# Strassen quads for v and z2, attention during the x load, and engine orders fixed at build time by a clock model

## The chip, the cores and the metric

The kernel runs on one core of one Trainium2 chip. The metric is the device time of one execution in microseconds (us). Times are medians of three or more executions. A ratio is the mean time of one kernel's runs over the mean of the other's runs of the same rounds, so it is not quite the ratio of the medians quoted beside it.

The engines are called as the profile calls them: PE is the tensor engine, PEld its weight loads, DVE the vector engine, ACT the scalar engine, SP the engine that issues most DMAs.

## The reference

The output is a gated mix of two branches over the same x (2048 rows, 1024 columns).

```python
# cut: random inputs; A_x (1, 2048, 1024), wqkv (1024, 3072), w_in (1024, 3584),
# w_sp (2048, 2048), w_out (1792, 1024): z1 and z2 have FH = 1792 columns each
g = _sigmoid((x * gate_w).sum(-1, keepdims=True))
a = _A_ref(x, A_wqkv, A_wo)                          # 32 heads of 32, local attention
b = _B_ref(x, B_w_in, B_w_sp, B_b_sp, B_w_out)
return g * a + (1 - g) * b

# _A_ref: q, k, v = x @ wqkv; every position attends to itself and to the 7 positions
# 2, 4, ... 14 before it; softmax of 8 logits; o @ wo
# _B_ref: z = gelu(x @ w_in); z1, z2 = halves of z; z2 = layernorm(z2);
# b = (z1 * (w_sp @ z2 + b_sp)) @ w_out
```

## The kernel before

The work in PE's order is: transposes of the first x tiles and a first quarter of z2 while x is still landing; the gate; for eight groups of four heads q and k, and the band products q·k of a group between them; v; the rest of z2; then z1, the spatial product and the output product. The last three were already done by Strassen's scheme, 7 products for 8; one such set of 7 is called a "quad" below. Attention after the bands is DVE's: it waits for the group's rows of logits, which go from SBUF to a DRAM scratch (`band_d`) and come back in another layout (`att_L`).

```python
# the products that the change replaces (cut: stores, counters)

    def z2_tile(i, c, bank=next_bank):
        N = ZC + 1 if c == 0 else ZC
        ps = bank()
        for kt in range(KT):
            nc.tensor.matmul(ps[:, 0:N], xT[:, kt, i * P:(i + 1) * P], w2[:, kt, w2_off[c]:w2_off[c] + N],
                             start=(kt == 0), stop=(kt == KT - 1))
    # ... cut

    def v_tile(hf, j):
        ps = low_bank()
        for kt in range(KT):
            nc.tensor.matmul(ps[:], _sub_ap(xT_flat, kt * S + j, [[NJ, P]]), wv[:, kt, 512 * hf:512 * hf + 512],
                             start=(kt == 0), stop=(kt == KT - 1))
        st = vst_slots[(j // 4) % 2]
    # ... cut: the v tile is copied by ACT and stored to v_d

# the band products and the copies that free their banks (cut: the loops over blocks and heads)
                    nc.tensor.matmul(banks[4 + h][QB * q:QB * (q + 1), m * KW + skip:(m + 1) * KW], qt[hp, e, at:at + QB],
                                     kt_[hp, e, at - (W - 1) + skip:at + QB], start=True, stop=True,
                                     tile_position=(DH * h, QB * q), skip_group_check=True)
    # ...
        evac = nc.scalar.copy(dst, src)
    # ... then DMAs from SBUF to band_d

# softmax of one group: rows come back, maxima on DVE, exponential on ACT
    def attend1(g):
        L = att_L[g % 2]
        L4 = L[:].rearrange("p (j u h) -> p j u h", j=NJ, u=W)
        bd = band_d[g]
        for e in range(2):
            sync.dma_start(L[:, 256 * e:256 * e + 256].rearrange("p (j x) -> p j x", j=8),
                           bass.AP(tensor=bd.tensor, offset=bd.offset + 16 * e * BS, ap=[[8 * (BR + HG), P], [BR + HG, 8], [1, W * HG]]))
        tt = nc.vector.tensor_tensor
        tt(att_m[:], L4[:, :, 0:4, :], L4[:, :, 4:8, :], ALU.max)
        tt(att_m[:, :, 0:2, :], att_m[:, :, 0:2, :], att_m[:, :, 2:4, :], ALU.max)
        tt(att_m[:, :, 0:1, :], att_m[:, :, 0:1, :], att_m[:, :, 1:2, :], ALU.max)
        last_sub[0] = tt(L4, L4, att_m[:, :, 0:1, :].to_broadcast([P, NJ, W, HG]), ALU.subtract)
        exps[g] = nc.scalar.activation(L[:], L[:], ACT.Exp, scale=float(SCALE))
        if EXP_AFTER[g] < len(evacs):
            tc.add_manual_dep(exps[g].ins, evacs[EXP_AFTER[g]].ins.name, NOSYNC, reason="by then its logits are there")
```

`EXP_AFTER` is a hand-written list: the exponential of group g stands in ACT's order at the 20th, 27th, 51st ... copy that ACT makes. Everything else in the engine orders before z1 is left to the scheduler.

## Time and profile before

| | before |
|---|---|
| median of 3 runs | 683.04 us (682.75 to 685.5) |
| profiled span | 680.2 us |
| PE busy | 665.4 us, 98% |
| first z1 product | 289.1 us |
| all that PE waited for anything | about 9 us, 5.8 of it for the first x rows |

From the page of the kernel before: busy times, PE's busy tenths in 40 equal slices of the span, the clock granted to PE in tenths, and the chain of waits.

```profile
span 680.2 us, 10313 instructions
...
PE 665.4 (98%) x4075; PEld 323.0 (47%) x4135; DVE 407.4 (60%) x551; ACT 289.5 (43%) x547; POOL 6.1 (1%) x15
...
PE   6999999999999999999999999999999999999997
...
PEclk9999999999999999999999999999999999999999
...
## 4 chain that ended last, share of the span: by engine, by line
PE 95%; DMA 2%; issue 1%; DVE 1%; SPq 1%; ACT 0%; ACTq 0%; DVEq 0%
```

From PE's waits, kernel before (what was waited for: us in total, times, longest).

```profile
engine line waited for: us in total, times, longest us
PE psum_all L202 <- DMA arena<-in_A_x_dram: 5.8, 2, 3.5
```

PE is the limit everywhere: it is busy in every slice, its clock is full, and it is 95% of the chain. Beyond the 9 us of waits, nothing but less PE work can shorten this kernel. From PE's timeline, kernel before, round the start of z1 (start us, us, operation, count):

```profile
start us, us, engine line op out<-in xcount [idle before <-releaser]
267.78 20.40 PE L232 MATMUL psum_all<-arena 128*128 128x448 bf16 x107
...
289.10 3.18 PE L474 MATMUL psum_all<-arena 128*128 128x512 bf16 x14
```

A run of 107 products of 448 columns takes 20.40 us, 0.191 each; PE goes from z2 into z1 without a gap. (Some matmul records are missing from the trace, so counts there can be short by a few per cent.)

### The profile page before, as it was taken

How to read it: one execution, taken by the hardware profiler on the slowest of the kernel's cores; microseconds unless marked ns; L12 is line 12 of the kernel's file. 1: busy time of each engine (PE TensorE's matmuls, PEld its weight loads, DVE VectorE, ACT ScalarE, POOL GpSimd, SP SyncE). 2: the span in 40 equal slices, each digit the busy share in tenths (PEclk: the TensorE clock that was granted, in tenths of full speed). 3: DMA queues.
4: the chain of work that ended last, by engine and by line, in shares of the span. 5: the costliest groups of instructions: out<-in, count | busy, mean ns of one | idle time of the engine just before them, and what ended most of it. 6: DMA issues, size and time to landing. Idle time of an engine off the chain costs nothing.

```text
span 680.2 us, 10313 instructions
## 1 busy us (share of the span) xinstructions
PE 665.4 (98%) x4075; PEld 323.0 (47%) x4135; DVE 407.4 (60%) x551; ACT 289.5 (43%) x547; POOL 6.1 (1%) x15
## 2 busy tenths in 40 slices
PE   6999999999999999999999999999999999999997
PEld 3544654466444555544444444444444444444443
DVE  1000119899199989866769766888676695333301
ACT  4435634624566889677866311212112122222221
POOL 1000000000000000000100000000000000000000
PEclk9999999999999999999999999999999999999999
DMA  9995654764666470138894587648356299944100
GB/s 232 225 277 116 139 137 116 167 172 94 155 177 154 126 163 1 52 104 191 210 187 155 140 195 153 151 129 255 95 149 167 67 208 187 212 106 98 46 32 31
DMA packets 241743, 98.12 MB, mean 144 GB/s; under 512 B 189712, under 2 KB 235168, under 8 KB 241696
## 3 DMA queue, kind: packets, MB, share of 16 engines
q1 hardware_dynamic: 241008, 96.94, 58.2%
q8 instruction: 32, 0.52, 0.3%
q10 hardware_dynamic: 688, 0.53, 0.2%
q14 instruction: 15, 0.12, 0.1%
HBM read 45.10 MB, written 36.61 MB: 120 GB/s over the span
## 4 chain that ended last, share of the span: by engine, by line
PE 95%; DMA 2%; issue 1%; DVE 1%; SPq 1%; ACT 0%; ACTq 0%; DVEq 0%
PE psum_all L474 56%; PE psum_all L272 16%; PE psum_all L232 15%; PE psum_all L280 6%; PE psum_all L312 2%; DMA band_d_71<-arena 1%; DMA arena<-in_A_x_dram 1%; SPq L184 0%; DMA arena<-o_d 0%; DMA v_d<-arena 0%; PE psum_all L202 0%; DVE arena L685 0%; ACT arena L283 0%; DVE arena L680 0%; DVE arena L525 0%
## 5 line engine op out<-in xcount | busy, mean ns | idle before, releaser
L474 PE MATMUL psum_all<-arena 128*128 128x512 f16 (+1 forms) x1758 | 385.6, 379 | 2.0 <-DVE arena L685 0.2
L474 PEld LDWEIGHTS <-arena 128*128 128x128 f16 (+1 forms) x1792 | 175.3, 98 | 212.2 <-issue 1.3
L272 PE MATMUL psum_all<-arena 128*128 128x512 bf16 x493 | 111.0, 379 | 2.3 <-issue 1.9
L232 PE MATMUL psum_all<-arena 128*128 128x448 bf16 (+1 forms) x512 | 99.7, 355 | 0.0
L365 DVE TENSOR_TENSOR arena<-arena,att_A 128x8192 f16<-128x8192 bf16 x16 | 70.7, 4420 | 12.1 <-DMA arena<-v_d 12.0
L272 PEld LDWEIGHTS <-arena 128*128 128x128 bf16 x512 | 48.6, 98 | 56.8 <-issue 0.2
L232 PEld LDWEIGHTS <-arena 128*128 128x128 bf16 x512 | 49.8, 98 | 47.0 <-issue 1.5
L365 DVE TENSOR_TENSOR arena<-arena 128x4096 f16<-128x4096 f16 (+2 forms) x48 | 67.3, 1401 | 1.2
L274 ACT CAST arena<-psum_all 128x512 bf16<-128x512 f32 x64 | 37.4, 586 | 53.3 <-PE psum_all L272 53.3
L280 PE MATMUL psum_all<-arena 128*128 128x512 bf16 x249 | 55.4, 379 | 0.9 <-issue 0.4
L483 ACT COPY psum_all<-psum_all 128x512 f32<-128x512 f32 x36 | 20.5, 570 | 80.7 <-PE psum_all L474 80.7
L523 DVE TENSOR_TENSOR arena<-arena 128x512 f16<-128x512 bf16 (+2 forms) x37 | 20.7, 568 | 42.1 <-PE psum_all L474 30.9
L234 ACT ACTIVATE arena<-psum_all 128x448 bf16<-128x448 f32 x64 | 34.7, 547 | 26.2 <-PE psum_all L232 26.0
L280 PEld LDWEIGHTS <-arena 128*128 128x128 bf16 x256 | 36.7, 144 | 18.5 <-issue 0.5
L497 ACT COPY psum_all<-psum_all 128x512 f32<-128x512 f32 x36 | 20.6, 571 | 48.7 <-PE psum_all L474 48.6
L490 ACT COPY psum_all<-psum_all 128x512 f32<-128x512 f32 x36 | 20.5, 570 | 48.6 <-PE psum_all L474 48.3
L590 ACT ACTIVATE arena<-psum_all 128x512 bf16<-128x512 f32 x56 | 31.6, 599 | 7.2 <-DVE psum_all L593 3.7
L319 ACT CAST arena<-psum_all 128x1988 f16<-128x1988 f32 (+1 forms) x24 | 33.7, 1405 | 1.1 <-PE psum_all L312 0.4
L526 DVE TENSOR_TENSOR arena<-arena 128x512 f16<-128x512 bf16 (+2 forms) x37 | 20.6, 566 | 21.2 <-PE psum_all L474 15.5
L338 DVE TENSOR_TENSOR att_m<-att_L_106 128x256 f16<-128x256 f16 x4 | 1.2, 290 | 50.8 <-DMA att_L_106<-band_d_68 32.8
L283 ACT CAST arena<-psum_all 128x512 bf16<-128x512 f32 x32 | 18.4, 587 | 26.5 <-PE psum_all L280 25.9
L487 ACT COPY arena<-psum_all 128x512 f32<-128x512 f32 x22 | 12.8, 587 | 34.5 <-PE psum_all L474 33.7
(87 smaller groups left out, 361.5 us busy)
## 6 DMA issues: line engine op xcount, KB each, us to landing
arena<-v_d SPq DMA_DIRECT2D x8, 960.0 KB, 6.9
z_d<-arena SPq DMA_DIRECT2D x28, 256.0 KB, 2.6
arena<-z_d SPq DMA_DIRECT2D x28, 256.0 KB, 3.3
zg_d<-arena SPq DMA_DIRECT2D x56, 128.0 KB, 2.2
arena<-zg_d SPq DMA_DIRECT2D x32, 224.0 KB, 3.1
arena<-in_A_wqkv_dram SPq DMA_DIRECT2D x16, 256.0 KB, 5.6
v_d<-arena SPq DMA_DIRECT2D x32, 128.0 KB, 2.4
o_d<-arena SPq DMA_DIRECT2D x4, 1024.0 KB, 5.5
```

The lines of the kernel that those rows point to most:

```text
L232: nc.tensor.matmul(ps[:, 0:N], xT[:, kt, i * P:(i + 1) * P], w2[:, kt, w2_off[c]:w2_off[c] + N], start=(kt == 0), stop=(kt == KT - 1))
L234: inst = nc.scalar.activation(z2[:, i, ZC * c:ZC * (c + 1)], ps[:, 0:ZC], ACT.Gelu_apprx_tanh, accum_out=s1[:, 4 * i + c:4 * i + c + 1])
L272: nc.tensor.matmul(ps[:], w[:, t, kt, :], xT[:, kt, 512 * c:512 * (c + 1)], start=(kt == 0), stop=(kt == KT - 1))
L274: inst = nc.scalar.copy(dst[:, :, 256 * c:256 * (c + 1)], ps[:].rearrange("p (n e) -> p e n", e=2))
L280: nc.tensor.matmul(ps[:], _sub_ap(xT_flat, kt * S + j, [[NJ, P]]), wv[:, kt, 512 * hf:512 * hf + 512], start=(kt == 0), stop=(kt == KT - 1))
L319: evac = nc.scalar.copy(dst, src)
L365: inst = nc.vector.tensor_tensor(*a)
L474: nc.tensor.matmul(bank[:], lhsT, rhs, start=(start and m == 0), stop=(stop and m == n - 1), skip_group_check=True)
L497: seed = nc.scalar.copy(V[:], Y[:])
L523: first = nc.vector.tensor_tensor(s_out[0], a21, a22, ALU.add)
L526: nc.vector.tensor_tensor(s_out[2], a11, a21, ALU.subtract)
L590: last_gelu[0] = nc.scalar.activation(z1s[:, f, a, :], bank[:], ACT.Gelu_apprx_tanh)
```

## The change

The intent is to take PE work away. v of groups 3 to 7 and almost all of z2 are now computed by Strassen quads on differences of x tiles. These differences were needed for z1 anyway and are now made at the start and kept. The v of groups 0 to 2 (with the gate column beside it, 385 columns in all) is computed during the x load, together with group 0's q, k and bands, so that attention starts earlier and DVE finds time for the quads' additions. And from the gate on the program is written in the order of a model of the engines, the "clock": every piece of work advances its engine's clock by a guessed duration, DMAs by a guessed issue, transfer and landing time, and the next thing to be written is whatever the model says is ready first. Each instruction is then tied to the one written before it on its engine, so that the scheduler can't move it ("pinned").

The diff is 1261 lines; this is its core. First, the placement of the exponentials and the old v and z2 go, and the model comes (cut marks are "# ..."):

```diff
# ...
-    EXP_AFTER = (20, 27, 51, 60, 83, 93, 103, 117)
# ...
+    pinned = {}
+    traced = [0]
+    due = []
+
+    def settle():
+        ins = nc.cur_bb.bb.instructions
+        for i in ins[traced[0]:]:
+            if i.engine in pinned:
+                if pinned[i.engine] is not None:
+                    tc.add_manual_dep(i, pinned[i.engine], NOSYNC, reason="as it is written")
+                pinned[i.engine] = i.name
+        traced[0] = len(ins)
+
+    def take(engine, dur, ready=0.0):
+        clock[engine] = max(clock[engine], ready) + dur
+        return clock[engine]
# ...
+    def issue(item):
+        if item in due:
+            due.remove(item)
+            ready, dur, f, landed = item
+            sp = take("SP", 0.55, ready)
+            end = take("DMA", dur, sp + 0.6) + 0.5
+            f()
+            if landed is not None:
+                landed(end)
+
# ...
```

The rows of a group are read back (`load_bands`) when the model says that its band stores have landed and DVE is done with the buffer; their landing time sets `t_bands`, which the maxima on DVE wait for in the model, and the end of the maxima sets the exponential's place in ACT's order:

```diff
# ...
+            L4 = att_L[g % 2][:].rearrange("p (j u h) -> p j u h", j=NJ, u=W)
+            yield lambda g=g: t_bands[g], 0.21, lambda: tt(att_m[:], L4[:, :, 0:4, :], L4[:, :, 4:8, :], ALU.max), False
+            yield now, 0.14, lambda: tt(att_m[:, :, 0:2, :], att_m[:, :, 0:2, :], att_m[:, :, 2:4, :], ALU.max), True
+            yield now, 0.11, lambda: tt(att_m[:, :, 0:1, :], att_m[:, :, 0:1, :], att_m[:, :, 1:2, :], ALU.max), True
+            yield now, 0.34, lambda: tt(L4, L4, att_m[:, :, 0:1, :].to_broadcast([P, NJ, W, HG]), ALU.subtract), True
+            sub_end[g] = clock["DVE"]
# ...
+    def next_bands():
+        g = bands_at[0]
+        if g < bands_have[0] and g - weighed[0] < 2 and not any(i in due for s in stored.values() for i in s):
+            dma(max(band_data[g], clock["DVE"] if g > 1 else 0.0), 0.9, lambda: load_bands(g), lambda t: t_bands.__setitem__(g, t))
+            take("SP", 0.6)
+            bands_at[0] += 1
# ...
+            events = [(max(i[0], clock["SP"]), 0, i) for i in due]
+            events += [(sub_end[g], 1, g) for g in range(NG) if sub_end[g] < FAR]
+            events += [(max(o[0], clock["DVE"]) + FR * o[1], 2 + n, o) for n, o in enumerate(options())]
+            events = [v for v in events if v[0] <= t]
# ...
+            elif kind == 1:
+                exp_end[x] = take("ACT", 0.6 + table("exp"), sub_end[x] + 0.1)
+                sub_end[x] = FAR
+                exponential(x)
# ...
```

The weights of z2 are loaded in 16 small DMAs of 112 KB per half, written as 8 events, spread by `gap` on the model's clock, and DVE's weight sums follow their landing:

```diff
# ...
+    def load_later(p, at, gap):
+        land = [0.0]
+
+        def landed(t):
+            land[0] += 1
+            if land[0] == KT:
+                fill.extend((t, 1.05, f) for f in wz_sums(p))
+        for n, f in enumerate(load_wz(p)):
+            dma(at + gap * n, 0.65, f, landed)
# ...
+            next_v()
+            load_later(0, clock["PE"] + 6.0, 3.0)
# ...
+    load_later(1, clock["PE"], 1.2)
+    mark(banks[4:8], ZC)
+    junk = reg(R_OFF + 12288, FH)
# ...
```

And in the start, the gate column's copy (it frees the PSUM bank of a v tile) goes from ACT to DVE:

```diff
# ...
-            nc.scalar.copy(gl_s[:, i:i + 1], ps[:, ZC:ZC + 1])
# ...
+        nc.vector.tensor_copy(gl_s[:, i:i + 1], ps[:, VP:VP + 1])
# ...
```

## The prediction

> **What bounds it now.** The tensor engine: the page shows PE busy 665.4 of 680.2 us, the chain of waits is 95% PE, and the view of waits gives PE only 9 us of waits, 5.8 of them for the first x rows. In the timeline a 512-column matmul costs 0.215 us start to start (1.727 per eight), a 448-column one 0.190 (62.3 us for 328). [...]
>
> **What changes.**
> - z2: 512 matmuls of 448 columns become 420 (15 quads) + 32: 97.3 -> 85.9 us.
> - v: 256 of 512 columns (55 us) become 128 of 385 (20.9) and 224 of 320 (30.5): 51.4 us.
> - Filler matmuls: 4 -> 16, +0.9 us.
> - q/k (110 us), bands, z1, spatial and output products stay.
>
> PE work before z1 falls by about 14 us, all on the critical path: the floor is 669 us.
>
> DVE gets weight sums (8 us for z2) and the bank additions of the v and z2 quads (12 and 22 us). With the attention (8 groups of 17 us of products and 2.5 of softmax) that is about 198 us, to fit in some 218 between its first softmax and z1. It fits because attention starts earlier (first maximum before: 69.9 us; after: 55 to 62). ACT in z1 loses copies and gains squares: neutral.
>
> **What I think is given back.**
> 1. Start, 5 us (2 to 8). In the built order of DVE the eight x differences stand between the tiny copies of the gate column (psum to gl_s) of x tiles 3 to 6, and a sum that waits for the late v weights stands before tile 7's. [...] The differences wait for x tiles 8-11 and 12-15. Transposed x loads are issued 1.62 us apart and land 3.9 us later; with the 512 KB q/k load put between (2.2 us at 232 GB/s), tile 11 lands near 22.5 us and tile 15 near 29. Tile 3's copy holds the bank that the first band products need at about 20 us; tiles 4-7 hold the four low banks. I expect PE to stall some 4 us at 20-25 us and 2 us at 30-37. Before, PE ran without a gap from 15.65 us.
> 2. z1 to spatial, 2 us: the last normalisation stands behind spatial weight sums (2.29 us each), and the first spatial sums behind it.
> 3. 1 us in the v and z2 quads, where an addition waits behind a 2.2 us attention product.
>
> Sum: 683 - 14 + 5 + 2 + 1 = 677 us.
>
> **What would show it.** 0.136 us per 320-column and 0.190 per 448-column matmul; first z1 product near 280 us (289.1 before); spatial and output stages still 167 and 137 us apart from step 2; PE waiting for DVE before 40 us and at the first spatial quad.
>
> **What would make it wrong.** If x lands sooner, the start costs nothing: 670. If DVE falls behind its fixed order in the z2 quads, or a store fixed behind a late load holds a band buffer, stalls add up to 683 or worse. [...]
>
> 677 us, range 670 to 683.5; chances 0.09 faster, 0.89 within 2%, 0.02 slower.

The 0.136 and 0.163 us of the new widths: scaling the 0.190 us of 448 columns by width, an estimate, gives the same two (0.190 x 320 / 448 and 0.190 x 385 / 448), so v comes to 128 x 0.163 + 224 x 0.136 = 51.4 us, and the 14 us are 11.4 of z2 and 3.6 of v, less 0.9 for the fillers.

## More of the kernel before

The kernel before was timed again beside every experiment, on three chips, and had medians of 682.5 to 684.25 us there; where half a per cent matters, read the ratios.

A band set's product fills four PSUM banks, and ACT has to copy them out before the next set may start. This copy and the exponential of the softmax are both ACT's.

## The result, and the profile after

| | before | after |
|---|---|---|
| median | 683.48 us (682.75 to 685.5, 4 runs) | 701.37 us (699.57 to 704.21, 4 runs) |
| ratio | | 1.0262, 95% interval 1.0232 to 1.0293 |
| profiled span | 680.2 us | 699.1 us |
| PE busy | 665.4 us | 663.4 us |
| DVE busy | 407.4 us | 455.6 us |
| mean clock granted to PE | 0.999 | 0.993 |

It is slower by 2.6%, 17.9 us in the medians, where I had given "slower" a chance of 0.02. The page after, the same lines as before:

```profile
span 699.1 us, 10783 instructions
...
PE 663.4 (95%) x4183; PEld 317.2 (45%) x4183; DVE 455.6 (65%) x668; ACT 291.4 (42%) x601; POOL 6.8 (1%) x15
...
PE   6899998997998799999999999999999999999997
...
PEclk9999999998999999999999999999999999999999
...
## 4 chain that ended last, share of the span: by engine, by line
PE 54%; issue 6%; DVE 5%; ACT 3%; DMA 1%; POOL 0%; POOLq 0%; DVEq 0%; ACTq 0%
```

PE now has slices of 7 and 8 tenths up to 250 us, its share of the chain fell from 95% to 54%, and in one slice (near 165 us) the clock falls below full. From PE's waits, kernel after:

```profile
engine line waited for: us in total, times, longest us
PE psum_all L339 <- ACT arena L347: 10.9, 7, 5.8
PE psum_all L212 <- DMA arena<-in_A_x_dram: 5.9, 2, 4.1
PE psum_all L405 <- ACT psum_all L500: 3.5, 1, 3.5
PE psum_all L405 <- ACT psum_all L423: 2.2, 2, 2.0
PE psum_all L339 <- DVE gl_s L299: 1.9, 1, 1.9
PE psum_all L375 <- DVE gl_s L299: 1.4, 1, 1.4
PE psum_all L405 <- DVE arena L541: 1.3, 1, 1.3
```

The line to be read is the first: a band product (L339) waited seven times, once for 5.8 us, for the copy (L347) by which ACT empties the banks of the set before it. In the kernel before the same wait does not appear, although ACT sat idle there too ahead of its exponentials (7.4 us); PE never waited for that.

**The stages.** PE's timeline after, where z2 ends and z1 begins:

```profile
269.79 31.19 PE L405 MATMUL psum_all<-arena 128*128 128x448 f16 x164
301.14 0.28 PE L550 MATMUL psum_all<-arena 128*128 128x64 bf16 x4 [0.16 <-ACT arena L773]
301.25 4.61 PE L405 MATMUL psum_all<-arena 128*128 128x512 bf16 x22
```

z1's first product starts at 301.25 us, but 20 products of the last z2 quad (3.8 us) are still mixed in with it. Like for like, z1 starts at about 305.3 us, 16.2 us later than before. Adding up PE's matmuls at their dense pace gives 13.6 us less work ahead of z1 than before. So 29.8 us were lost on the way, which I split at the gate product, 53.83 us after and 36.06 before: the work ahead of it adds up to 39.5 and 28.6 us, so 14.3 us of the start are no work after and 7.5 before.

| part (us, after minus before) | predicted | found |
|---|---|---|
| PE work ahead of z1 | -14 | -13.6 |
| start, up to the gate | +5 (2 to 8) | +6.8 |
| bands, v quads, z2 quads | +1 | +23.0 |
| z1 to the end | +2 | +2.7 |
| sum | -6 | +18.9 (span 699.1 - 680.2) |

The third row is off by 22.0 us, of 24.9 for the whole sum.

**What one hold is made of.** A hold is a stretch in which PE stands still for another engine. The longest, in the kernel after, as PE's timeline shows it (the bracket is the idle time just before, and who ended it):

```profile
start us, us, engine line op out<-in xcount [idle before <-releaser]
...
154.63 1.90 PE L288 MATMUL psum_all<-arena 128*128 128x512 bf16 x8
162.36 0.74 PE L339 MATMUL psum_all<-arena 32*64 32x71 bf16 x56 [5.83 <-ACT arena L347]
163.03 3.59 PE L288 MATMUL psum_all<-arena 128*128 128x512 bf16 x8
```

ACT's timeline of the same stretch:

```profile
152.96 0.58 ACT L347 CAST arena<-psum_all 128x512 f16<-128x512 f32 x1
159.49 0.63 ACT L622 ACTIVATE att_L<-att_L 128x512 f16<-128x512 f16 x1 [5.95 <-DVE att_L L634]
160.03 0.57 ACT L291 CAST arena<-psum_all 128x512 bf16<-128x512 f32 x1
160.49 1.82 ACT L347 CAST arena<-psum_all 128x1988 f16<-128x1988 f32 x1
```

ACT had copied the small first set of bands out at 152.96. The next band copy, the one that PE needs, stands in its order behind an exponential (L622), and this exponential waited 5.95 us for DVE's maxima. PE had finished the set that this copy empties by 154.7 us. The copy ran only at 160.49, behind the exponential and a q/k copy, and PE's next band set began as it ended, at 162.36. DVE:

```profile
142.12 0.69 DVE L675 TENSOR_TENSOR arena<-arena 128x1024 bf16<-128x1024 f16 x1
158.22 0.29 DVE L631 TENSOR_TENSOR att_m<-att_L 128x256 f16<-128x256 f16 x1 [15.40 <-DMA att_L<-band_d]
```

DVE was not busy. It stood 15.40 us at the first maximum, for the rows to come back from DRAM. And SP's queue:

```profile
145.43 1.69 SPq L196 DMA_DIRECT2D band_d<-arena  x2
147.18 3.78 SPq L196 DMA_DIRECT2D arena<-in_B_w_in_dram  x4
151.00 5.14 SPq L196 DMA_DIRECT2D att_L<-band_d  x2
```

The stores of the bands (145.43 to 147.1) are followed by four z2 weight loads, which take 3.78 us to issue, then by the two DMAs that read the rows back, which take 5.14 us; the first maximum starts at 158.22. The DMA engines were over 90% busy from 151 to 154 us, and the two read-backs of 64 KB took 4.2 us each to land. The model's own clock, which counts from the gate and can be read by adding a print to the kernel's build, had these rows landed at 93.5 us and the exponential done at 96.0; in the trace, counted from 54.1 us, the first maximum started at 104.1 and the exponential ended at 106.0. For the rows of the last group the model is 17.6 us early (157.7 against 175.3).

The late rows reach PE through DVE's order as well. The second longest hold of the kernel after, 3.54 us up to 231.98, starts with DVE standing at the last group's first maximum (L631), with the addition of a z2 quad (L466) behind it, a gelu on ACT behind that, and behind the gelu the bank copy (L500) that PE waits for:

```profile
229.51 0.29 DVE L631 TENSOR_TENSOR att_m<-att_L 128x256 f16<-128x256 f16 x1 [4.53 <-DMA att_L<-band_d]
...
230.21 0.62 DVE L466 TENSOR_TENSOR psum_all<-psum_all,arena 128x448 f32<-128x448 f32 x1
...
230.86 0.54 ACT L773 ACTIVATE arena<-psum_all 128x448 bf16<-128x448 f32 x1 [4.84 <-DVE psum_all L466]
```

All eight exponentials together, kernel after (what ACT sat idle for ahead of them: us, times):

```profile
  DVE att_L L634: 13.6, 5
```

That is ACT standing 13.6 us in all. What stood behind it waited too: in the timeline above the band copy, ready at 154.7 us, ran only at 160.49, behind the exponential.

**The second price of a hold.** After the hold of 5.83 us, 8 q/k products took 3.59 us, where the 8 just before took 1.90. Two holds of the z2 stage, PE's timeline after:

```profile
211.63 0.64 PE L339 MATMUL psum_all<-arena 32*64 32x71 bf16 x56 [2.73 <-ACT arena L347]
212.21 1.69 PE L780 MATMUL psum_all<-arena 128*128 128x448 bf16 x8
...
231.98 3.80 PE L405 MATMUL psum_all<-arena 128*128 128x448 bf16 x12 [3.54 <-ACT psum_all L500]
```

After 2.73 us of waiting 8 products of 448 columns took 1.69 us, the dense time; after 3.54 us 12 of them took 3.80, against 2.4 dense. The granted clock was 0.50 from 159.7 to 166.5 us and from 231.4 to 234.8. The length of the hold did not decide it alone. In the profiles of all runs, from 14 us on, the products after every hold of 3.25 us and more ran slower than dense, but so did those after holds of 2.19 us (e2: 72 of 448 columns took 15.46 us, 13.8 dense), 2.39 (e1: 8 of 448 took 3.05, 1.69 dense) and 2.77 (e6: 8 of 512 took 2.69, 1.90 dense), while after one of 3.19 us (e9) and the 2.73 us above 8 of 448 took 1.69. The two long holds of the change cost 1.7 and 1.4 us more than their own length, which my sum had no term for.

Holds of over 0.2 us between the gate and z1 add up to 18.3 us and the lost clock to 3.1, of the 23.0 + 4.2 us (the kernel before lost 4.2 there too, in small gaps).

### The profile page after: what moved, and what is told of

Read it like the earlier page. It is cut to its first block, busy times and chain, and to the rows that moved or that the text cites. A ratio compares the mean times of both kernels' runs of the same rounds, so it can differ in the third digit from the quotient of the medians.

```text
span 699.1 us, 10783 instructions
## 1 busy us (share of the span) xinstructions
PE 663.4 (95%) x4183; PEld 317.2 (45%) x4183; DVE 455.6 (65%) x668; ACT 291.4 (42%) x601; POOL 6.8 (1%) x15
## 4 chain that ended last, share of the span: by engine, by line
PE 54%; issue 6%; DVE 5%; ACT 3%; DMA 1%; POOL 0%; POOLq 0%; DVEq 0%; ACTq 0%
PE psum_all L405 54%; DVE psum_all L466 1%; DVE arena L926 1%; ACT arena L773 1%; DVE arena L668 1%; DMA att_L<-band_d 1%; ACT arena L347 1%; DMA arena<-o_d 0%; POOL rstd L923 0%; DVE arena L670 0%; ACT psum_all L500 0%; PE psum_all L550 0%; ACT L773 0%; ACT L622 0%; DVE arena L543 0%
## 5 line engine op out<-in xcount | busy, mean ns | idle before, releaser
L405 PE MATMUL psum_all<-arena 128*128 128x512 f16 (+5 forms) x2436 | 501.2, 368 | 9.6 <-ACT psum_all L500 3.5
L405 PEld LDWEIGHTS <-arena 128*128 128x128 f16 (+1 forms) x2436 | 238.1, 98 | 271.3 <-issue 13.8
L288 PE MATMUL psum_all<-arena 128*128 128x512 bf16 x512 | 116.3, 383 | 1.0 <-DVE gl_s L299 0.9
L288 PEld LDWEIGHTS <-arena 128*128 128x128 bf16 x512 | 48.9, 99 | 59.0 <-issue 4.0
L668 DVE TENSOR_TENSOR arena<-arena,att_A 128x4096 f16<-128x4096 bf16 x32 | 72.4, 2286 | 0.2
L423 ACT COPY psum_all<-psum_all 128x512 f32<-128x512 f32 (+1 forms) x30 | 15.8, 528 | 80.5 <-PE psum_all L405 78.7
L541 DVE TENSOR_TENSOR arena<-arena 128x512 f16<-128x512 bf16 (+3 forms) x38 | 21.5, 573 | 42.4 <-PE psum_all L405 30.7
L466 DVE TENSOR_TENSOR psum_all<-psum_all,arena 128x448 f32<-128x448 f32 (+1 forms) x58 | 37.4, 660 | 12.3 <-PE psum_all L405 8.1
L670 DVE TENSOR_TENSOR arena<-arena 128x4096 f16<-128x4096 f16 x16 | 36.6, 2286 | 0.2
L543 DVE TENSOR_TENSOR arena<-arena 128x512 f16<-128x512 bf16 (+3 forms) x38 | 21.5, 570 | 23.3 <-PE psum_all L405 12.4
L347 ACT CAST arena<-psum_all 128x1988 f16<-128x1988 f32 (+3 forms) x25 | 33.9, 1355 | 5.2 <-PE psum_all L339 2.6
L444 ACT COPY psum_all<-psum_all 128x512 f32<-128x512 f32 (+1 forms) x30 | 15.9, 529 | 46.2 <-PE psum_all L405 45.2
L434 ACT COPY psum_all<-psum_all 128x512 f32<-128x512 f32 (+1 forms) x30 | 15.8, 528 | 40.5 <-PE psum_all L405 39.9
L339 PE MATMUL psum_all<-arena 32*64 32x71 bf16 (+1 forms) x1024 | 12.7, 207 | 13.1 <-ACT arena L347 10.9
L631 DVE TENSOR_TENSOR att_m<-att_L 128x256 f16<-128x256 f16 x8 | 2.3, 292 | 34.3 <-DMA att_L<-band_d 34.3
```

What stands on the lines that cost most here:

```text
L288: nc.tensor.matmul(ps[:], w[:, t, kt, :], xT[:, kt, 512 * c:512 * (c + 1)], start=(kt == 0), stop=(kt == KT - 1))
L405: nc.tensor.matmul(bank[:, 0:N], lhsT, rhs, start=(start and m == 0), stop=(m == n - 1), skip_group_check=True)
L466: last_add[0] = nc.vector.tensor_tensor(out[:, n], a[:, n], vs, ALU.add)
L541: first = nc.vector.tensor_tensor(s_out[0], a21, a22, ALU.add)
L668: lambda ws=ws, in0=in0, in1=in1: tt(p5[:, ws], in0[:, ws], in1[:, ws], ALU.mult)), False
L670: yield now, 2.2, lambda: tt(p3[:, 0:4, :], p3[:, 0:4, :], p3[:, 4:8, :], ALU.add), True
```

## The experiments

My theory after reading the traces: ACT is held at exponentials whose place was fixed on the model's word, the rows come later than the model says, because the z2 weight loads share SP's queue and the DMA engines with them, and so the banks of the bands aren't freed. Its rivals: (a) the start, which shifted everything; (b) pinning as such, so that the scheduler alone would do better; (c) the model's price for the loads; (d) VectorE standing at its own fixed places (maxima, weight sums) rather than ACT at the exponentials; (e) the Strassen chains being less than dense. The last falls with the traces alone as far as the pace goes: 148 products of 320 columns took 20.26 us in a stretch without a hold, 0.137 each. The waits of the quads for copies and additions are among the holds counted above.

All experiments are edits of the changed kernel. All but one gave the right result. "ACT at exp" is the time that ACT sat idle ahead of the eight exponentials, whatever ended it, from its source line in each trace.

| run | median us | ratio to before (95%) | ACT at exp us |
|---|---|---|---|
| the change | 701.37 | 1.0262 (1.0232 to 1.0293) | 13.6 |
| e1 gate copy on ACT | 699.2 | 1.0232 (1.0189 to 1.0274) | 11.3 |
| e2 rows 6 us later | 697.96 | 1.0215, wrong result | 18.5 |
| e3 unpinned | 708.28 | 1.0367 (1.0332 to 1.0402) | 22.6 |
| e4 dearer loads in the model | 702.62 | 1.0279 (1.0244 to 1.0314) | 14.0 |
| e5 loads thinned | 699.57 | 1.0240 (1.0203 to 1.0277) | 15.8 |
| e6 start mended | 697.58 | 1.0216 (1.0183 to 1.0249) | 15.6 |
| e7 start, loads | 695.46 | 1.0190 (1.0151 to 1.0229) | 15.2 |
| e8 start, loads, rows 3 us later | 684.3 | 1.0016 (0.9987 to 1.0045) | 2.0 |
| e9 rows 3 us later | 699.7 | 1.0212 (1.0175 to 1.0249) | 8.2 |
| e10 start, rows 3 us later | 695.01 | 1.0150 (1.0112 to 1.0188) | 11.9 |
| e11 start, loads, rows 3 us (group 6: 9) | 679.39 | 0.9929 (0.9898 to 0.9959) | 1.6 |
| e12 the same with 4.5 and 9 us | 682.16 | 0.9962 (0.9935 to 0.9989) | 2.7 |
| e13 e11 without the start | 683.79 | 1.0000 (0.9977 to 1.0023) | 1.8 |
| e14 e11 without the thinned loads | 693.9 | 1.0150 (1.0123 to 1.0177) | 9.6 |
| e15 exponentials alone 6 us later | 701.99 | 1.0272 (1.0251 to 1.0294) | 6.6 |

The last column already tells most of it: the four kernels with at most 2.7 us there run in 679 to 684 us, the rest in 694 or more. Among the rest it does not order the times: e15 has 6.6 us there and no gain, as is told below. The intervals of e1, e2, e4, e5, e6, e9 and e15 overlap that of the change, so a gain of up to 4 us that one of them shows alone is of the size of the noise.

### e1: the gate column's copy back on ACT

```diff
-        nc.vector.tensor_copy(gl_s[:, i:i + 1], ps[:, VP:VP + 1])
+        nc.scalar.copy(gl_s[:, i:i + 1], ps[:, VP:VP + 1])
```

> Edit: the copy of the gate column out of each v bank goes to ACT instead of DVE, so it no longer stands behind the x differences. In the trace of the changed kernel PE reaches the first product after the gate (the 72 q/k matmuls of group 1) at 54.1 us, against about 47 us if it lost no more than the kernel before did. Theory A (the start costs 7 us because the eight x differences hold the gate copies and so the banks): that point comes at 47 to 49 us. What of it reaches the end is open: theory A1 (stalls are independent): 694 to 696 us in all. Theory A2 (the band and v data are bound by the loads, so the group 0 softmax still begins near 62 us and the later waits grow): 698 to 702 us in all.

699.2 us. The waits for DVE at the start are gone, but a new one takes their place, from PE's timeline of e1:

```profile
40.41 6.12 PE L288 MATMUL psum_all<-arena 128*128 128x512 bf16 x14 [4.18 <-ACT gl_s L299]
```

ACT now stood with the copy of a v tile behind the store of an earlier one, which SP had queued after the tail of the start-up loads. 14 products after it took 6.12 us for 3.2, the page of e1 shows a granted clock of 8 tenths in that slice (35.0 to 52.5 us), and the gate product came at 57.2 us instead of 53.8. Taking one waiter away exposed the next.

### e2: the rows of every group 6 us later in the model

```diff
-  ... lambda t: t_bands.__setitem__(g, t))
+  ... lambda t: t_bands.__setitem__(g, t + 6.0))
```

> Edit: the clock model that fixes the orders is told that the band rows land 6 us later than it believed; so the softmax maxima, the exponentials and what follows are placed later in the fixed orders. Theory B (PE stalls because an exponential stands in the ACT order before its rows have landed, and the band copies behind it hold the banks: 5.8 us at 156-162 us, 2.7 at 209, 7 us at 224-256, and a granted clock of 0.93 after it): the wait of PE for the band copies falls from 10.9 us to under 3, the first z1 product comes at 291 to 297 us instead of 305, total 685 to 692 us. Rival C (Strassen quads lose time in their chain of bank copies, wherever the exponentials stand): no change within 2 us, 699 to 704. Rival D (DVE is full, so later maxima only move the wait to the end of the z2 quads): 697 to 702, with PE waiting for DVE in the last quads.

The result was wrong, 7.6% relative error, so its time of 697.96 us is only a hint. ACT still stood 18.5 us at exponentials, but hardly ahead of band copies any more: the waits for these fell to 0.7 us. Instead a hold of 4.25 us came at 167 us, where q/k products waited for their copies, behind an exponential at which ACT stood 9.38 us. PE also waited 4.8 us for additions of the z2 quads and 2.2 us for another DVE result, as the rival that DVE becomes the limit had foretold, and its time range (697 to 702) was met. The likely cause of the wrong result, argued and not shown by a run of its own: the scratch that receives the squares lies in the memory of a v buffer of group 6. The program order decides which comes first, and with the later rows the squares are written ahead of attention's last reads. No race, only a wrong program: in this design the correctness of the order rests on the model as well. In e8 to e15 that scratch was moved (to `R_OFF + 39360`, half as long); all of those that place rows or exponentials later came out right.

### e3: the same order, not pinned

```diff
     for inst in (gate_mm, gate_act, gate_vec, gate_dma):
-        pinned[inst.ins.engine] = inst.ins.name
+        pass
```

Without the first four pins no later instruction is tied to the one before it on its engine.

> Edit: the clock model still decides in which order the instructions are written, but the pins that hold each engine to it are left out; the framework's scheduler orders the engines, as in the kernel before. Rival E (fixing the orders is what costs): 685 to 692 us. Theory B (where the exponentials are written decides, and the scheduler keeps nearly that place, as its built order shows): 697 to 706 us.

708.28 us, 1% slower than the change, and ACT stands 22.6 us at exponentials. Leaving out the pins gains nothing: rival (b) falls. Without them ACT's exponentials still stand within five copies of their pinned places (q/k and band copies counted in both traces), while DVE's order differs much more; the waits are spread otherwise (5.5 us at the bands, 4.8 and 4.5 in the quads, 4.3 at q/k copies).

### e4: a dearer pair of loads in the model

```diff
-            sp = take("SP", 0.55, ready)
+            sp = take("SP", 0.55 * n, ready)        # n = 2 for the pairs of weight loads
-            dma(at + gap * n, 0.65, f, landed)
+            dma(at + gap * n, 1.3, f, landed, 2)
```

> Edit: in the clock model a load of z2 weights counts as two issues of 0.55 us and 1.3 us of transfer instead of one issue and 0.65 us (the trace shows two issues of 0.55 to 1 us each for 230 KB), and a q/k load as two issues. Theory B1 (these loads, standing in the queue between the stores of the bands and their read back, are what the model undersized): exponentials 3 and 7 move later, PE waits for the band copies under 6 us, total 688 to 696. If the shift of the order is too small to matter: 697 to 702.

702.62 us, no gain; holds of 4.11 us at 161 us and 7.49 at 217. The model of the change is wrong by 10 us and more from group 3 on, and this repair did not close that (7 to 15 us there): rival (c), as a repair of this one price, does not carry it.

### e5: the z2 weight loads thinned out

```diff
-            load_later(0, clock["PE"] + 6.0, 3.0)
+            load_later(0, clock["PE"] + 6.0, 6.0)
-    load_later(1, clock["PE"], 1.2)
+    load_later(1, clock["PE"] + 10.0, 1.2)
```

> Edit: the loads of the z2 weights are thinned out: the first half is spread over 48 us instead of 24, the second begins 10 us later, after the bands of group 7. Nothing else moves by design. Theory B1 (the weight loads in the one queue delay the stores and the reading back of the bands, and so the exponentials that ACT is held to): group 3's rows, read 14.7 us after its last band copy in the changed kernel, come in under 11; the waits of PE for band copies at 156-162 and 209 us fall under 2 us each, the one of 3.5 us after 228 goes; first z1 product at 292 to 297 us (305), total 686 to 692. Rival F (the rows are late because every stage of the attention is late against the clock model after the slow start, whatever else is loaded): under 3 us gained, 697 to 702.

699.57 us. The hold at 160 us fell from 5.83 to 3.42 us, and another of 5.61 came at 212.8, where ACT waited 4.86 us for another group's exponential. The rows of group 3 came 12.3 us after its last band copy, against 14.7 before and the 11 that I had asked for. Loads alone are worth 1.8 us, inside the noise, and the time is the one that my rival F had foretold (697 to 702), not mine.

### e6: the start mended

The gate copy on ACT as in e1, and the loads that no one needs early (group 2's q/k weights, the zeros, v's second weights) taken from the tail of the start-up queue and issued after the v tiles 4 to 7, so that the v stores are not behind them:

```diff
-    for m in range(2):
-        first_dma(wvr[m], wq_v[:, :, 2 * D + VP + VH * m:2 * D + VP + VH * (m + 1)])
-    load_wqk(2, first_dma)
-    first_dma(... zeros)
# ... and in the loop over c, after vp_tile(i, low_bank):
+        if c == 1:
+            load_wqk(2, first_dma)
+            first_dma(... zeros)
+            for m in range(2):
+                first_dma(wvr[m], wq_v[:, :, 2 * D + VP + VH * m:2 * D + VP + VH * (m + 1)])
```

> Edit: the start alone, both of its holds: the gate copies go to ACT, and the stores of v stand in the queue before the third q/k load, the zero rows and the late v weights instead of behind them (in e1 ACT stood 4.2 us at x tile 8 for the buffer that those stores free, and the granted clock fell after it). Theory A (7 us of the start are these two holds): the first q/k product after the gate at 47 to 50 us (54.1). If the rest keeps its distance to it (A1): total 692 to 696. If the rest is bound by late rows (A2): 698 to 702.

697.58 us. The gate product comes at 49.96 us, 3.9 us earlier, and PE's waits for the gate column fall from 4.2 to 1.0 us. The total gains 3.8 us. The holds at the bands stay (6.25, 2.77 and 1.84 us). Rival (a) is right for about 4 us and for no more.

### e7 and e8: start and loads; and the rows 3 us later too

e7 joins e5 and e6. e8 adds the later rows of e2 with 3 us, and the moved scratch.

> Edit: e5 and e6 together. If the two causes are separate their gains add: 679 to 687 us.

> Edit: e7, and the clock model is told that band rows land 3 us later; the scratch output of the squares is moved off the v buffer, which in e2 was still in use (hence its wrong result). Theory B: what is left of PE waiting for band copies goes, 677 to 685 us. Rival D (DVE becomes the limit): PE waits for DVE 3 to 6 us in the last z2 quads, 682 to 690.

695.46 and 684.3 us; e7 missed its forecast of added gains by 8 us. The step from e7 to e8 is 11.2 us, where I had no edit so far that gave more than 4. In e8 ACT stands 2.0 us at exponentials instead of 15.2. One hold of 3.33 us is left, at 199.5 us, where ACT loads its table for exp and again for gelu, 1.28 us each, between two band copies.

### e9 and e10: the rows 3 us later, alone and with the start

> Edit: only the 3 us of later band rows in the clock model (and the scratch output of the squares moved to a free place), start and weight loads as in the changed kernel. e7 to e8 showed 11 us for this edit. If the place of the exponentials is the main cause by itself: 687 to 692 us, PE waiting for band copies under 4 us (10.9). If it works only together with an early start or thin weight loads: 695 to 700.

> Edit: e8 without the thinned weight loads (mended start plus 3 us later rows). If the weight loads do not matter (e5 gained nothing): 683 to 686 us, as e8. If they do: 687 us or more.

699.7 and 695.01 us. Later rows alone are worth 1.7 us, and with the start but dense loads the holds of 4.60 and 5.58 us are back, with ACT standing 8.2 us (e9) and 11.9 us (e10) at exponentials. So 3 us of slack are enough only where the loads leave the rows alone.

### e11 and e12: the best combination

e11 is e8 with 9 us for group 6, whose exponential was the last hold; e12 has 4.5 us for the others.

```diff
-  ... lambda t: t_bands.__setitem__(g, t))
+  ... lambda t: t_bands.__setitem__(g, t + (9.0 if g == 6 else 3.0)))
```

> Edit: e8, and the rows of group 6 are told 9 us late instead of 3, so that its exponential and two loads of an activation table (1.28 us each) leave the place between the first Gelus and the last two band copies, where PE stood 3.3 us in e8 and then ran at about half clock for 3 us. If that is right: PE's waits near 195 us under 1 us, total 678 to 681 us, faster than the kernel before. If the wait only moves into the z2 quads: 683 to 686.

> Edit: as e11 with 4.5 us instead of 3 for the other groups, for the waits of 0.5 and 1.3 us that e8 kept at groups 4 and 5. 676 to 680 us if DVE still has the room; 680 to 685 us, with more PE waiting for DVE in the z2 quads, if it has not.

e11 runs in 679.39 us (678.83 to 680.94), ratio 0.9929 (0.9898 to 0.9959): it beats the kernel before by 0.7% and the change by 22.0 us, and its result is right. PE's waits in e11, and what ACT sat idle for ahead of the exponentials:

```profile
PE psum_all L208 <- DMA arena<-in_A_x_dram: 6.0, 2, 4.2
PE psum_all L335 <- ACT arena L343: 2.0, 5, 0.9
```

```profile
  DVE att_L L635: 1.6, 3
```

The waits at the bands (here L335) fell from 10.9 to 2.0 us, none over 0.93, and the mean granted clock is 1.000: after holds this short e11 lost no clock. e12 at 682.16 us shows that more slack isn't better: DVE then reaches its additions in the z2 quads late (PE waits 2.7 us for them, 0.5 in e11).

### e13 and e14: one part taken out of the best

> The best version (679.4 us) with the start as the changed kernel had it. If the start's gain adds to the others' without regard to them: gate back at about 54 us (4 us later), time 682 to 687. If its gain exists only because it shifts the later stages against the weight loads (the gains are not additive), holds of over 3 us come back at the bands and the time is 690 or more.

> The best version with the z2 weight loads as dense as the changed kernel issues them. If the loads between a group's band store and its read-back are needed to explain the late rows: rows of groups 3 and 4 land later again, a hold of 3 to 6 us at the bands before 180 us, 686 to 695 us. If the later place of the exponentials alone suffices: 679 to 683.

e13 (old start) runs in 683.79 us, 4.4 us more than e11. The start is worth 3.8 us alone (e6), 4.1 on top of the loads (e7 against e5) and 4.4 on top of all: it adds to the rest. That settles rival (a).

e14 (dense loads) runs in 693.9 us, 14.5 more than e11. Its trace shows by what way the loads come in. DVE's timeline of e14:

```profile
155.68 4.23 DVE L538 TENSOR_TENSOR arena<-arena 128x1792 f16<-128x1792 bf16 x4 [4.56 <-DMA arena<-in_B_w_in_dram]
```

and PE's:

```profile
168.36 0.74 PE L335 MATMUL psum_all<-arena 32*64 32x71 bf16 x56 [4.42 <-ACT arena L343]
```

DVE stood 4.56 us at its first weight sum (L538) for the loads, then did four sums and two attention products that are written ahead of the maxima; ACT stood 4.54 us for those maxima and PE 4.42 us for ACT. So a fixed order on DVE hands a late load on to ACT and from there to PE. A longer hold of e14 doesn't pass through an exponential at all:

```profile
227.31 24.20 PE L406 MATMUL psum_all<-arena 128*128 128x448 f16 x112 [5.70 <-DVE psum_all L467]
```

DVE had stood 5.47 us at another weight sum for its load, with the addition (L467) of a z2 quad behind it. PE waited 8.0 us for such additions in e14, and 0.5 in e11.

### e15: the exponentials alone

The exponential's place in ACT's order 6 us later, the maxima on DVE where they were, the scratch moved:

```diff
-            events += [(sub_end[g], 1, g) for g in range(NG) if sub_end[g] < FAR]
+            events += [(sub_end[g] + 6.0, 1, g) for g in range(NG) if sub_end[g] < FAR]
# ...
-                exp_end[x] = take("ACT", 0.6 + table("exp"), sub_end[x] + 0.1)
+                exp_end[x] = take("ACT", 0.6 + table("exp"), sub_end[x] + 6.1)
```

> The changed kernel with nothing but the exponential's place in the fixed order of ScalarE moved 6 us later (the maxima on VectorE stay; what depends on the exponential follows; the squares' scratch is moved so that nothing is overwritten). If the holds come from ScalarE standing at an exponential whose rows are late, the hold of 5.8 us at 162 us falls below 2.5 us and the time is 690 to 696. If VectorE's standing at the maxima is as much to blame, holds move to VectorE or to other bands and the time stays at 697 to 702.

701.99 us, so the time that my theory in its narrow form asked for (690 to 696) was missed. PE's timeline of e15:

```profile
153.96 0.64 PE L339 MATMUL psum_all<-arena 32*64 32x71 bf16 x56 [0.23 <-ACT arena L347]
...
208.68 0.74 PE L339 MATMUL psum_all<-arena 32*64 32x71 bf16 x56 [8.20 <-ACT arena L347]
209.35 3.17 PE L780 MATMUL psum_all<-arena 128*128 128x448 bf16 x8
```

The hold of the change at 162 us is gone, as the theory said (0.23 us at that band set). But a band set of the last group waited 8.20 us, and ACT's timeline says why:

```profile
206.81 1.82 ACT L347 CAST arena<-psum_all 128x1988 f16<-128x1988 f32 x1 [8.04 <-DMA band_d<-arena]
```

This time ACT itself stands at the band copy, for the store of the set whose SBUF buffer it reuses. In that stretch an attention output of 1 MB, a v load of 960 KB and four band stores had been issued within 6 us, the DMA engines were mostly 90% busy or more, and a band store took 8.8 us to land (median of six; 5.2 for four in the change at 186 to 214 us). After it came a wait of 4.0 us for DVE's additions. What follows: the exponential's place, with what depends on it, is the cause of the hold at 162 us, since moving it removes the hold. It is not the cause of all of them, and the next hold in line took the gain. Rival (d) is right in part: DVE's fixed order passes delays on (the 3.54 us hold of the change, e14, e15), and the DMA's load does too. The later rows of e8 to e14 move the maxima and the exponentials together, so how much of their gain belongs to each engine is not shown. Why exactly these transfers met in e15 I did not test.

### Taken together

With S for the start, W for the thinned loads and R for later rows (3 us, group 6 9 us): R and W without S, e13, gain 17.6 us on the change; W alone gains 1.8, R with uniform 3 us alone 1.7 (R with the 9 us was not run alone). S adds 4.4. The two that don't add are two ends of one path: W makes the rows come sooner, R makes the order expect them later. The model's own times bear this out: from group 3 on the exponentials end 10 to 17 us later than the model has them in the change, and in e13 all eight end within 1.1 us of it. As long as the rows miss their fixed places on DVE and ACT by more than the slack, each miss costs its hold and, for the two longest of the change, 1.7 and 1.4 us of clock besides, and a miss removed lets PE and so the stores and loads of the next group arrive in another pattern, with the next miss.

## Why the prediction was wrong

- **PE work: right.** Predicted 14 us less ahead of z1, found 13.6. 320 columns were estimated at 0.136 us and took 0.137, tail included (148 in 20.26 us); 448 columns take 0.191, as before.
- **Start: right in cause, 1.8 us short.** I predicted 5 us (2 to 8) from copies of the gate column standing behind x differences on DVE. The waits for `gl_s` are there, mainly at 23.6, 39.3 and 53.8 us (1.9, 0.7 and 1.4 us), though smaller and in part later than I had placed them. Found: 6.8 us, of which these waits are 4.2; where the rest went I did not trace. Mending it gave back 3.8 to 4.4 us (e6, e13).
- **z1 to spatial: right.** Predicted 2 us, found 1.25 for the wait named (L405 for DVE's L541 sums) and 2.7 for the whole stretch to the end.
- **"3. 1 us in the v and z2 quads, where an addition waits behind a 2.2 us attention product": this is the step that failed.** The term measured 23.0 us. About half of it, 10.9 us, is not even in the quads but in the bands, among the q/k products and the last plain z2 products, which the sum had no term for; and the longest hold in the quads, 3.54 us, came from DVE standing 4.53 us for late rows, not from a 2.2 us product. Three things were left out. First, I checked that DVE's work fits (198 us in 218) and took that for enough; DVE idled 15.4 us at one maximum, with room to spare, because the rows were late. An engine that has time in total can still be late at a fixed place. Second, ACT: I wrote "ACT in z1 loses copies and gains squares: neutral" and did not ask what stands in ACT's order between two band copies. The built order showed the exponentials there, and the trace of the kernel before had the durations of stores and read-back from which the slack could have been worked out. Third, the clock: the two longest holds cost 1.7 and 1.4 us more.
- **The warning was right and got no weight.** "If DVE falls behind its fixed order in the z2 quads, or a store fixed behind a late load holds a band buffer, stalls add up to 683 or worse" is nearly what happened: a read-back fixed among loads held the band's banks and, once, a quad's addition, and in e15 a store did hold a band buffer. I gave "slower" a chance of 0.02 without having worked out the arrival of a single group's rows.

What stays open: what the model would need to be right by itself (e4's one price was not it); why the transfers of e15 met; and about 10 us between e11 and the 669 us floor of the prediction. In e11's trace some 3 us of it are the start, 2 the bands, and 3 the stretch after z1; the rest is spread over small waits.

## What to carry to other kernels

Where several engines run orders that are fixed at build time, an engine's total of busy time says little: for each instruction that waits for a DMA, work out when its data arrive, and look at what stands behind it in the same queue. Put a consumer of late data behind the work that others are waiting for, with a few microseconds of slack, and keep the loads that share its queue from eating the slack. And when a removed wait gains nothing, look for the next one in line before giving up the cause: thinned loads and 3 us of slack gained under 2 us each, and the two together (with 9 us for one group) 17.6.
